# Moving the output-projection load, joining two transposes and splitting the gate/up tasks in a fused linear-attention and GEGLU kernel

## The chip, the cores and the metric

The kernel runs on one core of a Trainium2 chip. Its engines are TensorE (PE in the profile; its weight loads are the row PEld), VectorE (DVE), ScalarE (ACT), GpSimd (POOL) and SyncE (SP), which here only issues DMA transfers. The metric is device microseconds (us) of one execution; each version is told by the median of several runs.

## The reference

The input x has 2048 tokens of 448 numbers in bfloat16. The block is linear attention with 16 heads of 28 and then a gated MLP, each behind a layer norm without weights and each with a residual:

```python
def phi(t): return where(t > 0, t + 1, exp(t)) + 1e-6
q, k, v = split(layernorm(x) @ wqkv)          # 16 heads of 28
kv  = einsum("bhsd,bhse->bhde", phi(k), v)    # summed over all tokens
z   = phi(k).sum(tokens)
o   = (phi(q) @ kv) / (phi(q) @ z + 1e-6)
h   = x + o @ wo
g, u = layernorm(h) @ w_gate, layernorm(h) @ w_up      # 448 -> 1792
out = h + (gelu(g) * u) @ w_down                        # 1792 -> 448
```

Since kv and z are sums over all tokens, no token's o can be computed before all keys and values are there. That splits the program in two halves.

## The kernel before

**Tiles.** The tokens are 16 tiles t of 128. In the first half a tile is normed (`norm t`, on DVE for tiles 0 to 3, on POOL for the rest), transposed into `xnT`, and projected. Tiles 0 to 3 are transposed by TensorE (`tr0` to `tr3`, L495) and copied out of PSUM by ACT (`ev0` to `ev3`, L523); tiles 4 to 15 by a DMA transpose that SP issues (`xT4` to `xT15`, L526). Projection is `k t` and `v t`, each a task of 8 or 6 matmuls of 448 columns. Then ACT takes the exponential (`ek t`, L565), `cl t` clamps it on POOL (L566), `ph t` on DVE makes phi(k) of it (L568), `evv t` on ACT copies v (L570), and `acc t a/b` adds phi(k) times v into two PSUM banks. The queries are projected in eight pairs of tasks `qa c h`, `qb c h` (chunk c of four tiles, half h); ACT and DVE make phi(q) of them (`eq`, `rq`, `cq`, `pq`, L616 to L627).

**Second half.** `kz1` and `kz2` (DVE, L642 and L643) copy the finished sums. `nd t` multiplies phi(q) by them, `rd t` and `om t` divide (L654, L655), the result `o_sb` is transposed into `oT`, `wo t` multiplies by wo, `hr t` adds the residual (L660), layer norm follows, its result `hn` is transposed into `hnT`, and `gu v` computes gate and up for one or two blocks of 128 of the 1792 columns; ACT takes the gelu (`ge`, L830), DVE multiplies (`hm`, L832), and `down` multiplies by w_down. Tiles 0 and 1 take a short way: TensorE transposes o (`tro0`, `tro1`, L681) and hn (`trh0`, `trh1`, L702). The others go by DMA transpose in pairs: `nd t a/b`, `oT`, `wo t a/b`, `hT`. The MLP runs over token chunks of 2, 2, 4, 4 and 4 tiles: gu0 to gu6, gu7 to gu13 (256 columns a matmul, two column blocks a task), then 14 tasks of 512 columns for each chunk of four tiles.

**Half-array matmuls.** Most tasks use matmuls of 64 rows that come in pairs, one on the upper rows of the array (A), one on the lower (B), each into its own PSUM bank; the two run beside each other (`pe_pairs`, L430). The `b` task of a pair writes the same two banks with the row halves exchanged, and so waits until the `a` task has left the array. Tasks nd0, nd1, tro, wo0, wo1, trh and down12 to down15 use all 128 rows.

**What sets the order.** Every engine runs its tasks in a list written out by hand in `ORDERS`, one string for each of PE, ACT, DVE, POOL and SP. The graph works out which tasks a task depends on, and each engine waits by semaphores (`wait_ge`) at the head of the task, or in the middle of it for tasks whose later matmuls alone need something. SP's queue before is: the loads of x and wqkv, xT4 to xT15, four loads of wo (`dwo`, `dwo_t`, `dwo_u`, `dwo_s`, 336, 56, 56 and 336 KB), fourteen of gate and up (`dwg`, `dwu`, 224 KB each), oT2, oT3, the load of w_down, and so on. At the start PE runs 16 small and `WARM = 38` larger matmuls on ones (`warm1`, `warm0`, L454), whose result nobody reads, while x is on its way. These are the lines that the prediction's steps touch:

```python
G.add("pe", warm_fn(WARM), r=[b_ones], w=bank(0), name="warm0", dur=WARM * 0.107, key=-100.0)
prev = xts[-1:]                                  # wo's first load stands behind xT15
op("pool", lambda e: e.tensor_scalar(tm1[:, ie, :], e1[:, ie, :], 1.0 + EPS, 0.0, ALU.min, ALU.max), ...)   # cl t
pe_pairs("gu%d" % v, both(a, b), N, ...)         # one task of 28 matmuls
```

Of the kernel before, what the change touches and what calls it, by code (L numbers as in the profile page):

```python
# [213 lines left out]
def _c_act(n):  # L214
    return 0.05 + n / 1200.0
# [15 lines left out]
def bass_sequential_preLN__linear_attn_block__glu_gated_geglu__prompt_kernel(  # L231
# [13 lines left out]
    QCH = 512  # L245
    NQC = S // QCH
    N_PE_TR = 4
    STAT_GROUPS = [[0], [1], [2], [3]] + [[t, t + 1] for t in range(4, T, 2)]
    EV_DVE = cfg.get("ev_dve", ())
    N_DVE_NORM = cfg.get("n_dve_norm", 4)  # L250
    N_PE_A2 = 2
# [661 lines left out]
```

## Time and profile before

| | us |
|---|---|
| median of three runs | 196.68 (196.21 to 196.73) |
| the profiled execution, its own time | 196.7 |
| its span, first to last instruction | 194.9 |
| PE busy | 190.3 (98%) |
| DVE busy | 116.3 (60%) |
| ACT busy | 78.2 (40%) |
| POOL busy | 42.0 (22%) |

The profile is one execution. 1.8 us of its own time lie outside its span. Times in the rows count from the span's start. Rows of a timeline give the start, the length, the engine, the line, the operation, what it writes and reads, and how many instructions were merged; in brackets stands how long the engine was idle before, and what ended it. PE's matmuls are pipelined, so rows of the same engine overlap by some 0.2 us, and the distance from one row's start to the next is the better measure of what a task costs.

### The profile page before, as it was taken

How to read it: one execution, taken by the hardware profiler on the slowest of the kernel's cores; microseconds unless marked ns; L12 is line 12 of the kernel's file. 1: busy time of each engine (PE TensorE's matmuls, PEld its weight loads, DVE VectorE, ACT ScalarE, POOL GpSimd, SP SyncE). 2: the span in 40 equal slices, each digit the busy share in tenths (PEclk: the TensorE clock that was granted, in tenths of full speed). 3: DMA queues.
4: the chain of work that ended last, by engine and by line, in shares of the span. 5: the costliest groups of instructions: out<-in, count | busy, mean ns of one | idle time of the engine just before them, and what ended most of it. 6: DMA issues, size and time to landing. Idle time of an engine off the chain costs nothing.

```text
span 194.9 us, 5336 instructions
## 1 busy us (share of the span) xinstructions
PE 190.3 (98%) x2192; PEld 137.9 (71%) x2192; DVE 116.3 (60%) x301; ACT 78.2 (40%) x205; POOL 42.0 (22%) x90
## 2 busy tenths in 40 slices
PE   7999999999999999999999999999999999999994
PEld 7556658754588977976675577877778779899554
DVE  2989735368998946843967745756735443431512
ACT  3689866669784212220442441233232442411100
POOL 3099974300050310500500500500500000000000
PEclk9999999999999999999999999999999999999999
DMA  6944558999836052152062250172040000010111
GB/s 191 377 116 97 81 110 185 247 248 205 260 103 110 15 101 50 50 105 62 10 129 46 46 106 2 30 117 51 5 94 28 23 0 0 3 47 3 47 47 47
DMA packets 37256, 17.53 MB, mean 90 GB/s; under 512 B 28272, under 2 KB 36336, under 8 KB 37232
## 3 DMA queue, kind: packets, MB, share of 16 engines
q1 hardware_dynamic: 36352, 16.45, 36.8%
q10 hardware_dynamic: 880, 0.75, 1.2%
q8 instruction: 17, 0.28, 0.6%
q14 instruction: 7, 0.06, 0.1%
HBM read 8.72 MB, written 1.84 MB: 54 GB/s over the span
## 4 chain that ended last, share of the span: by engine, by line
PE 96%; issue 1%; ACT 1%; DVE 1%; POOL 0%; DVEq 0%; ACTq 0%; POOLq 0%
PE ps L430 87%; PE ps L780 6%; PE ps L454 2%; DVE x_sb L660 1%; PE ps L495 1%; ACT xn L617 1%; PE ps L681 0%; ACT xnT L523 0%; PE ps L672 0%; DVE x_sb L756 0%; POOL ones_bf L395 0%; POOL eps_t L398 0%; ACT pqT L616 0%; DVEq L196 0%; ACTq L196 0%
## 5 line engine op out<-in xcount | busy, mean ns | idle before, releaser
L430 PE MATMUL ps<-hnT,wgu_sb 64*128 64x512 bf16 (+1 forms) x980 | 90.4, 333 | 0.0
L430 PEld LDWEIGHTS ps<-hnT,wgu_sb 64*128 64x128 bf16 x980 | 64.5, 94 | 18.6 <-DVE hh L832 1.7
L830 ACT ACTIVATE gl<-ps 128x256 bf16<-128x256 f32 x112 | 36.9, 381 | 89.3 <-PE ps L430 88.2
L832 DVE TENSOR_TENSOR hh<-ps,gl 128x256 bf16<-128x256 f32 x112 | 42.5, 415 | 35.7 <-ACT gl L830 31.5
L430 PE MATMUL ps<-wd_sb,hh 64*128 64x448 bf16 x336 | 34.4, 349 | 0.0
L430 PEld LDWEIGHTS ps<-wd_sb,hh 64*128 64x128 bf16 x336 | 25.6, 94 | 6.2 <-DVE x_sb L756 0.2
L430 PE MATMUL ps<-wkv_sb,xnT 64*128 64x448 bf16 x192 | 22.4, 350 | 0.4 <-ACT xnT L523 0.4
L462 DVE BATCH_NORM_STATS2 st<-x_sb 128x6 f32<-128x448 bf16 x32 | 18.7, 611 | 2.6 <-DMA x_sb<-in_A_x_dram 2.6
L756 DVE TENSOR_TENSOR x_sb<-ps,x_sb 128x448 bf16<-128x448 f32 (+1 forms) x17 | 9.9, 591 | 16.6 <-PE ps L430 9.8
L474 POOL TENSOR_SCALAR ln<-mv 128x2 f32<-128x2 f32 x7 | 1.6, 223 | 75.0 <-DVE mv L463 74.9
L568 DVE SCALAR_TENSOR_TENSOR pk<-ps,tm 128x448 bf16<-128x448 f32 x16 | 9.8, 620 | 9.6 <-POOL tm L566 7.1
L430 PE MATMUL ps<-xnT,wq_sb 64*128 64x512 bf16 x112 | 14.9, 377 | 0.2 <-ACT xn L617 0.2
L430 PEld LDWEIGHTS ps<-wkv_sb,xnT 64*128 64x128 bf16 x192 | 10.1, 94 | 6.3 <-issue 0.8
L430 PE MATMUL ps<-wo_sb,oT 64*128 64x448 bf16 x98 | 12.1, 350 | 0.1
L660 DVE TENSOR_TENSOR x_sb<-ps,x_sb 128x448 bf16<-128x448 f32 x16 | 9.4, 618 | 4.6 <-PE ps L430 4.4
L780 PE MATMUL ps<-wd_sb,hh 128*128 128x448 bf16 (+1 forms) x70 | 10.8, 315 | 0.0
L566 POOL TENSOR_SCALAR tm<-e 128x448 bf16<-128x448 bf16 x16 | 8.9, 559 | 6.4 <-ACT e L565 5.5
L487 POOL TENSOR_SCALAR hn<-x_sb,nm,rs 128x448 bf16<-128x448 bf16 x14 | 10.0, 720 | 0.8 <-POOL rs L476 0.2
L565 ACT ACTIVATE e<-ps 128x448 bf16<-128x448 f32 x16 | 8.5, 541 | 3.5 <-PE ps L430 2.2
L780 PEld LDWEIGHTS ps<-wd_sb,hh 128*128 128x128 bf16 x70 | 6.7, 98 | 4.3 <-issue 0.4
L655 DVE TENSOR_TENSOR o_sb<-ps,rd 128x448 bf16<-128x448 f32 x16 | 9.4, 612 | 0.1
L570 ACT ACTIVATE v<-ps 128x448 bf16<-128x448 f32 x16 | 8.4, 542 | 2.1 <-PE ps L430 2.1
(69 smaller groups left out, 140.4 us busy)
## 6 DMA issues: line engine op xcount, KB each, us to landing
out_dram<-x_sb SPq DMA_DIRECT2D x15, 112.0 KB, 1.7
wgu_sb<-in_B_w_gate_dram SPq DMA_DIRECT2D x7, 224.0 KB, 6.1
wgu_sb<-in_B_w_up_dram SPq DMA_DIRECT2D x7, 224.0 KB, 6.4
wd_sb<-in_B_w_down_dram SPq DMA_DIRECT2D x1, 1568.0 KB, 8.3
x_sb<-in_A_x_dram SPq DMA_DIRECT2D x2, 448.0 KB, 5.3
wkv_sb<-in_A_wqkv_dram ACTq DMA_DIRECT2D x2, 336.0 KB, 3.7
x_sb<-in_A_x_dram SPq DMA_DIRECT2D x3, 224.0 KB, 4.2
wo_sb<-in_A_wo_dram SPq DMA_DIRECT2D x2, 336.0 KB, 4.4
```

Source lines behind the costliest of these rows:

```text
L430: ins = e.matmul(o_, l_, r_, start=s_, stop=p_, **kw)
L462: op("dve", lambda e: e.bn_stats(st[:, t, :], src_ap), [b_src], [b_st[t]], "%sbnst%d" % ("" if mv is mv1 else "h", t), 0.53, key, after=after)
L487: return lambda e: e.tensor_scalar(dst, src[:, t, :], nm[:, t:t + 1], rs[:, t:t + 1], ALU.add, ALU.mult)
L565: act_exp(lambda e: e.activation(e1[:, ie, :], oK, AF.Exp), bank(bk), [b_e1[ie]], "ek%d" % t, _c_act(D), kk)
L566: op("pool", lambda e: e.tensor_scalar(tm1[:, ie, :], e1[:, ie, :], 1.0 + EPS, 0.0, ALU.min, ALU.max), [b_e1[ie]], [b_tm1[ie]], "cl%d" % t ...
L568: op("dve", lambda e: e.scalar_tensor_tensor(pk[:, i, :, 0:GW], psK3, EPS, tm1[:, ie, :].rearrange("p (g e) -> p g e", g=NG), ALU.max, ALU ...
L655: op("dve", lambda e: e.tensor_tensor(o_sb[:, so, oc:oc + D].rearrange("p (a e) -> p a e", e=28), nd3[:, :, 0:28], rd[:, i, :].unsqueeze(2 ...
L660: op("dve", lambda e: e.tensor_tensor(h_sb[:, u, :], ps[:, b, 0:D], x_sb[:, u, :], ALU.add), bank(b) + [b_x[u]], [b_h[u]], "hr%d" % u, 0.5 ...
L756: op("dve", lambda e: e.tensor_tensor(x_sb[:, t, c0:c1], ps[:, bk, c0:c1], h_sb[:, t, c0:c1], ALU.add), bank(bk) + [b_h[t]], [bo], "out%d% ...
L780: ins = e.matmul(ps[:, bk, c0:c1], hh[:, j, hsl(t)], wd_sb[:, j, c0:c1], start=(j == 0), stop=(j == NJ - 1))
L830: G.add("act", lambda e, gi=gi, cs_=cs_, psG=psG: e.activation(gl[:, gi, cs_], psG[:, cs_], AF.Gelu_apprx_tanh), r=bank(BK_G[i]), w=[b_glh ...
L832: op("dve", lambda e, dst=dst, srcU=srcU, srcL=srcL: e.tensor_tensor(dst, srcU, srcL, ALU.mult), bank(BK_U[i]) + [b_glh], [b_ar[j_][t % HR ...
```

## The change

- `WARM` goes from 38 to 33.
- SP's queue: `dwo` and `dwo_t` stand behind xT9, `dwo_u` and `dwo_s` behind xT11; gate and up follow xT15 directly. `WO_AT = 3` lets wo's first load stand anywhere behind xT6.
- `cl14` and `cl15` run on DVE (`CL_DVE`).
- One task `tro0` takes the place of tro0 and tro1: it transposes o of both tiles by 16 transposes of 64 rows, A and B, into two banks; `evo0` and `evo1` each read both banks.
- In `trh` the wait for the copied columns (`wrap`) moves to the seventh transpose.
- The gate/up tasks of two column blocks (gu0 to gu13) become two tasks each, `gu v a` and `gu v b`, with 14 matmuls; their number in all, their banks and the work of ACT and DVE behind them stay.
- The five lists are written anew. Beside what the excerpts below show, PE's list has qa20 behind acc14a and down6 to down10 earlier among the gate/up tasks; ACT's has ek15 ahead of evv15 and rstd3 behind ek0 and ln4; POOL's has norm11 behind norm12; DVE's has pq8, pq12 and pq14 later, and hm33_0 behind hr14 and hr15; SP's has dout13 ahead of dout10, dout11, dout9 and dout12.

```diff
-    " qa20 acc13a acc14a qb20 acc14b acc15b acc15a qa11 nd0 nd1 qb11 qa30 nd2a tro0 nd2b qb30 qa21 tro1 qb21 wo1 wo0"
-    " qa31 wo2a qb31 wo2b trh1 trh0 nd4a nd4b gu1 gu0 gu3 gu2 gu5 wo4a wo4b gu4 nd6a gu7 nd6b gu6 down0a gu9 wo6a gu8"
+    " acc13a acc14a qa20 acc14b acc15b qb20 acc15a qa11 nd0 nd1 qb11 qa30 nd2a tro0 nd2b qb30 qa21 qb21 wo1 wo0 qa31"
+    " wo2a wo2b trh1 trh0 qb31 nd4a nd4b gu1a gu1b gu0a gu0b gu3a gu3b gu2a gu2b gu5a gu5b wo4a gu4a wo4b gu4b gu7a"
...
+    CL_DVE = cfg.get("cl_dve", (14, 15))
...
-    WARM = 38
+    WARM = 33
...
+    WO_AT = 3
...
-        prev = xts[-1:]
+        prev = xts[WO_AT:WO_AT + 1]
...
+        prev = prev + xts[-1:]
+
         for k in range(7):
...
-            op("pool", lambda e: e.tensor_scalar(tm1[:, ie, :], e1[:, ie, :], 1.0 + EPS, 0.0, ALU.min, ALU.max),
-               [b_e1[ie]], [b_tm1[ie]], "cl%d" % t, 0.53, kk)
+            op("dve" if t in CL_DVE else "pool", lambda e: e.tensor_scalar(tm1[:, ie, :], e1[:, ie, :], 1.0 + EPS, 0.0, ALU.min, ALU.max),
+               [b_e1[ie]], [b_tm1[ie]], "cl%d" % t, _c_dve(D, 4.0) if t in CL_DVE else 0.53, kk)
...
-            def ftro(e):
-                ins = None
-                for k in range(4):
-                    ins = e.transpose(tvo[:, k, :], o_sb[:, so, k * 128:(k + 1) * 128], ident[:])
-                return ins
-            G.add("pe", ftro, r=[b_o[so], b_ident], w=bank(bh), name="tro%d" % t, dur=_c_mm(128, 4), key=ka)
-            op("act", lambda e: e.activation(oT[:, so, :, :], tvo, AF.Identity), bank(bh), [b_oT[so]], "evo%d" % t, _c_act(512), ka)
+        def tro_first():
+
+            P, Q = FIRST_BK[0][1], FIRST_BK[1][1]
 
             def ftro(e):
                 ins = None
-                for k in range(4):
-                    ins = e.transpose(tvo[:, k, :], o_sb[:, so, k * 128:(k + 1) * 128], ident[:])
+                for t in (0, 1):
+                    for k in range(4):
+                        for b, rows in ((P, A_), (Q, B_)):
+                            ins = e.transpose(psb[:, b, (4 * t + k) * 64:(4 * t + k + 1) * 64], o_sb[rows, t % O_R, k * 128:(k + 1) * 128], ident[rows, rows])
                 return ins
+            G.add("pe", ftro, r=[b_o[0], b_o[1], b_ident], w=bank(P, Q), name="tro0", dur=0.054 * 8, key=-19.9, mode=64, rg={P: "A", Q: "B"})
+            for t in (0, 1):
+                tvo = psb[:, P:Q + 1, t * 256:(t + 1) * 256].rearrange("p b (k t) -> p k b t", t=64)
+                ov_ = oT[:, t % O_R, :, :].rearrange("p k (b t) -> p k b t", t=64)
+                op("act", lambda e, tvo=tvo, ov_=ov_: e.activation(ov_, tvo, AF.Identity), bank(P, Q), [b_oT[t % O_R]], "evo%d" % t, _c_act(512), -19.8)
...
-            G.add("pe", ftrh, r=[b_hn[sh], b_hnd[sh], b_ident], w=bank(bh), name="trh%d" % t, dur=_c_mm(128, 7), key=ka)
+            G.add("pe", ftrh, r=[b_hn[sh], (b_hnd[sh], 6), b_ident], w=bank(bh), name="trh%d" % t, dur=_c_mm(128, 7), key=ka, mw=True, pdt=_c_mm(128))
...
-                a, b = [], []
                 for jj in range(nj):
                     j = j0 + jj
+                    a, b = [], []
...
-                pe_pairs("gu%d" % v, both(a, b), N, [b_hnT[t % HR] for t in tiles] + [(x, 2 * k) for k, x in enumerate(b_wg)] + [(x, 2 * k + 1) for k, x in enumerate(b_wu)],
-                         [(b_ps[BK_G[i]], 0), (b_ps[BK_U[i]], 1)], kb, {BK_G[i]: "A", BK_U[i]: "B"})
+                    pe_pairs("gu%d%s" % (v, "ab"[jj] if nj > 1 else ""), both(a, b), N,
+                             [b_hnT[t % HR] for t in tiles] + [(x, 2 * k) for k, x in enumerate(b_wg)] + [(x, 2 * k + 1) for k, x in enumerate(b_wu)],
+                             [(b_ps[BK_G[i]], 0), (b_ps[BK_U[i]], 1)], kb + 0.01 * jj, {BK_G[i]: "A", BK_U[i]: "B"})
```

In SP's queue, from the last small load on (`pqT<-ones_bf`), before:

```order
L364 DMA pqT<-ones_bf 1x64x128
L526 DMA_TRANSPOSE xnT<-xn 128x4x128 x12
L364 DMA wo_sb<-in_A_wo_dram 128x3x448
L364 DMA wo_sb<-in_A_wo_dram 64x448 x2
L364 DMA wo_sb<-in_A_wo_dram 128x3x448
L364 DMA wgu_sb<-in_B_w_gate_dram 64x1792
```

and now (`xnT<-xn` are xT4 to xT15, `wo_sb` the four loads of wo):

```order
L367 DMA pqT<-ones_bf 1x64x128
L529 DMA_TRANSPOSE xnT<-xn 128x4x128 x6
L367 DMA wo_sb<-in_A_wo_dram 128x3x448
L367 DMA wo_sb<-in_A_wo_dram 64x448
L529 DMA_TRANSPOSE xnT<-xn 128x4x128 x2
L367 DMA wo_sb<-in_A_wo_dram 64x448
L367 DMA wo_sb<-in_A_wo_dram 128x3x448
L529 DMA_TRANSPOSE xnT<-xn 128x4x128 x4
L367 DMA wgu_sb<-in_B_w_gate_dram 64x1792
```

Six transposes stand behind loads that they stood ahead of, and the first load of gate and up follows the last transpose.

On PE, from nd0 and nd1 (`ps<-kvz,pqT` x8, 128 rows) to the first full-array matmuls of wo1, before (`xnT,wq_sb` are qa and qb, `ident,o_sb` is tro):

```order
L672 MATMUL ps<-kvz,pqT 128x116 x8
L430 MATMUL ps<-xnT,wq_sb 128x512 x14
L430 MATMUL ps<-kvz,pqT 128x116 x8
L681 MATMUL ps<-ident,o_sb 128x128 x4
L430 MATMUL ps<-kvz,pqT 128x116 x8
L430 MATMUL ps<-xnT,wq_sb 128x512 x14
L681 MATMUL ps<-ident,o_sb 128x128 x4
L430 MATMUL ps<-xnT,wq_sb 128x512 x6
L688 MATMUL ps<-wo_sb,oT 128x448 x3
```

and now:

```order
L676 MATMUL ps<-kvz,pqT 128x116 x8
L433 MATMUL ps<-xnT,wq_sb 128x512 x14
L433 MATMUL ps<-kvz,pqT 128x116 x8
L690 MATMUL ps<-ident,o_sb 128x64 x16
L433 MATMUL ps<-kvz,pqT 128x116 x8
L433 MATMUL ps<-xnT,wq_sb 128x512 x20
L706 MATMUL ps<-wo_sb,oT 128x448 x3
```

tro1 between qa21 and qb21 is gone, and the one tro0 stands between nd2a and nd2b.

On PE, from qa31 to the tasks behind wo4, before (`ident,hn` is trh, `kvz,pqT` x16 is nd4a and nd4b, `wo_sb,oT` are wo2 and then wo4, `hnT,wgu_sb` gate and up):

```order
L430 MATMUL ps<-xnT,wq_sb 128x512 x8
L430 MATMUL ps<-wo_sb,oT 128x448 x8
L430 MATMUL ps<-xnT,wq_sb 128x512 x6
L430 MATMUL ps<-wo_sb,oT 128x448 x6
L702 MATMUL ps<-ident,hn 128x128 x14
L430 MATMUL ps<-kvz,pqT 128x116 x16
L430 MATMUL ps<-hnT,wgu_sb 128x256 x140
L430 MATMUL ps<-wo_sb,oT 128x448 x14
L430 MATMUL ps<-hnT,wgu_sb 128x256 x28
```

and now:

```order
L433 MATMUL ps<-xnT,wq_sb 128x512 x8
L433 MATMUL ps<-wo_sb,oT 128x448 x14
L722 MATMUL ps<-ident,hn 128x128 x14
L433 MATMUL ps<-xnT,wq_sb 128x512 x6
L433 MATMUL ps<-kvz,pqT 128x116 x16
L433 MATMUL ps<-hnT,wgu_sb 128x256 x140
L433 MATMUL ps<-wo_sb,oT 128x448 x8
L433 MATMUL ps<-hnT,wgu_sb 128x256 x14
L433 MATMUL ps<-wo_sb,oT 128x448 x6
L433 MATMUL ps<-hnT,wgu_sb 128x256 x28
```

qb31 went from between wo2a and wo2b to behind trh0, and half of gu4 stands between wo4a and wo4b.

More of the change, by code (lines that the diff above doesn't have):

```diff
@@ L661, in res_h, with nd_first @@
             ln_stats(u, h_sb[:, u, :], b_h[u], st2, mv2, b_st2, b_mv2, ka)
-        def a2_first(t):
+        def nd_first(t):
             ka = -20.0 + 0.1 * t
-            bnd, bh = FIRST_BK[t]
-            so = t % O_R
+            bnd = FIRST_BK[t][0]
             def fnnd(e):
@@ L696, in a2_first, with ftrh @@
             tvh = psb[:, bh, 0:896].rearrange("p (k t) -> p k t", k=7)
-            def ftrh(e):
+            def ftrh(e, W):
                 ins = None
-                for k in (0, 1, 2, 4, 5, 6, 3):
+                for n, k in enumerate((0, 1, 2, 4, 5, 6, 3)):
+                    if n in (0, 6):
+                        W(n)
                     ko = k * 128 if k < 4 else (k - 4) * 128 + 64
@@ L837, in gu_chunk @@
             vcount[0] = v
+        for t in (0, 1):
+            nd_first(t)
+        tro_first()
         done = 0
```

5 lines of the change are left out of this document (4 added, 1 removed), and 91 rows, old and new, of the table ORDERS.

## The prediction

> **What bounds the kernel now.** I read the page first: the share of the span by engine, and the chain that ended last.
>
> ```profile
> PE 190.3 (98%) x2192; PEld 137.9 (71%) x2192; DVE 116.3 (60%) x301; ACT 78.2 (40%) x205; POOL 42.0 (22%) x90
> ...
> PE 96%; issue 1%; ACT 1%; DVE 1%; POOL 0%; DVEq 0%; ACTq 0%; POOLq 0%
> ```
>
> PE is busy for 98% of the span and is 96% of the chain. What can be won is the time before its first useful matmul and the few places where it waits. The chain in order of time says where these are:
>
> ```profile
> 10.51 27.04 PE ps L430 x336
> ...
> 48.05 1.03 ACT xn L617
> ...
> 52.26 1.17 DVE x_sb L660 x2
> ...
> 62.84 40.46 PE ps L430 x552
> ...
> 103.35 78.37 PE ps L430 x776
> ```
>
> Behind 62.84 PE runs on without a break that matters (40.46 and 78.37 us in single pieces), so from there a change of order wins nothing and can only lose. The time lies in three stretches: the start, 37 to 54 us, and wo4 at 62.
>
> **The start: five warm-up matmuls less.** The timeline of the start:
>
> ```profile
> 1.93 4.24 PE L454 MATMUL ps<-ones_bf 128*128 128x128 bf16 x38
> 5.21 0.37 DVE L486 TENSOR_SCALAR xn<-x_sb,mv,rs 128x448 bf16<-128x448 bf16 x1
> 6.10 0.96 PE L495 MATMUL ps<-ident,xn 64*128 64x64 bf16 x20
> 7.43 0.74 PE L430 MATMUL ps<-wkv_sb,xnT 64*128 64x448 bf16 x6 [0.36 <-ACT xnT L523]
> 9.76 0.75 PE L495 MATMUL ps<-ident,xn 64*128 64x64 bf16 x20
> 10.26 0.20 ACT L469 ACTIVATE rs<-ln 128x2 f32<-128x2 f32 x1
> 10.35 1.08 ACT L523 ACTIVATE xnT<-ps 128x512 bf16<-128x512 bf16 x2
> 10.99 0.31 PEld L430 LDWEIGHTS ps<-wkv_sb,xnT 64*128 64x128 bf16 x6 [0.26 <-ACT xnT L523]
> 11.00:20.00 9.00, 9.00 (x114) 5.15 (x114) 8.60 (x24) 8.22 (x27) 9.00 (x18) 1.00 0.41 83
> ```
>
> One warm-up matmul takes 4.24 / 38 = 0.11, five 0.53. But tr0 needs norm0, which ends at 5.21 + 0.37 = 5.58, so tr0 moves from 6.10 to about 5.65, and k0 from 7.43 to 6.98: 0.45 won. At k2 (10.99, idle 0.26) PE waits for ev2 (10.35). ACT's new list puts rstd3 ahead of it, at the price of rstd4, 10.35 - 10.26 = 0.09, so 0.35 arrives there. In the stretch from 11 to 20 (the last row: PE, PEld, DVE, ACT, POOL busy) POOL is busy for 9.00 of 9.00 us and DVE for 8.60, and PE gets its banks back only when they are done. POOL's share can begin some 0.25 earlier, as its input `ek1` does. Ends: 0 (POOL's row alone decides) and 0.45; I take 0.25.
>
> **wo between the transposes.** Nothing needs wo before wo1 at 47.02 (its row is below); what counts is who is moved past. SP's rows and the landing times of L526:
>
> ```profile
> 20.68 2.59 SPq L526 DMA_TRANSPOSE xnT<-xn  x2
> 23.47 1.19 SPq L526 DMA_TRANSPOSE xnT<-xn  x1
> 28.64 3.19 SPq L364 DMA_DIRECT2D wo_sb<-in_A_wo_dram  x4
> DMA to landing us min/median/max: 2.4/2.5/4.1
> 25.70 0.73 PE L430 MATMUL ps<-wkv_sb,xnT 64*128 64x448 bf16 x6
> 30.42 0.82 PE L430 MATMUL ps<-wkv_sb,xnT 64*128 64x448 bf16 x6
> ```
>
> xT10 is issued at 20.68 and lands 2.5 later, at 23.2; k10 reads it at 25.70. xT12 is issued at 23.47, lands near 26, and k12 reads it at 30.42. Four issues take 3.19. Two of them (1.9 with the long first one) now stand ahead of xT10, partly where SP waited anyway: I put xT10 at 22.0, landing at 24.5. All four stand ahead of xT12, and xT11 waits longer for norm11, which POOL now makes after norm12: xT12 at 25.9, landing at 28.4 to 30.0 (2.5 to 4.1). k10 and k12 come at 25.45 and 30.15. So the cover is 0.9 at k10 and 0.15 to 1.75 at k12, and I cost this at nothing; without the cover it is the first rival. Gate and up start behind xT15 without wo's 3.19 in between, so w_gate, w_up, oT2 and oT3 come no later.
>
> **37 to 41 us: cl14, cl15 and the order of acc.** The rows of POOL and DVE:
>
> ```profile
> 38.58 0.56 POOL L566 TENSOR_SCALAR tm<-e 128x448 bf16<-128x448 bf16 x1 [0.75 <-ACT e L565]
> 39.27 0.62 DVE L568 SCALAR_TENSOR_TENSOR pk<-ps,tm 128x448 bf16<-128x448 f32 x1 [0.68 <-PE ps L430]
> 40.62 0.63 DVE L642 TENSOR_TENSOR kvz<-ps,mask 113x448 bf16<-113x448 f32 x1 [0.73 <-PE ps L430]
> 41.24 0.42 DVE L618 TENSOR_SCALAR pqT<-pqT 112x1024 bf16<-112x1024 bf16 x1
> ```
>
> DVE's own clamp of 1024 numbers takes 0.42, so 448 take at most that; I take 0.35 against POOL's 0.56. With ek15 ahead of evv15 (0.4) and ph14 out of the way, ph15 comes some 0.9 earlier. Little of it counts: qa20 now waits for evv15, which is 0.4 later, and qb20 for qa20. Following the tasks one by one, the last acc leaves PE 0.2 earlier, kz1 (40.62) too. Won: 0.19; ends 0 and 0.5 (the 0.73 that DVE waits ahead of kz1, less what evv15 loses).
>
> **41 to 54 us: the joint transpose and qb31.**
>
> ```profile
> 43.78 0.40 PE L681 MATMUL ps<-ident,o_sb 128*128 128x128 bf16 x4
> 44.11 0.38 PE L430 MATMUL ps<-kvz,pqT 64*128 64x116 bf16 x8
> 45.94 0.40 PE L681 MATMUL ps<-ident,o_sb 128*128 128x128 bf16 x4
> 46.27 0.82 PE L430 MATMUL ps<-xnT,wq_sb 64*128 64x512 bf16 x6
> 47.02 0.74 PE L688 MATMUL ps<-wo_sb,oT 128*128 128x448 bf16 x3
> 49.21 1.04 PE L430 MATMUL ps<-xnT,wq_sb 64*128 64x512 bf16 x8 [0.19 <-ACT xn L617]
> 52.16 0.95 PE L702 MATMUL ps<-ident,hn 128*128 128x128 bf16 x14
> 53.47 0.82 PE L430 MATMUL ps<-kvz,pqT 49*128 49x116 bf16 x15 [0.21 <-DVE x_sb L660]
> 54.13 2.13 PE L430 MATMUL ps<-hnT,wgu_sb 64*128 64x256 bf16 x36
> ```
>
> tro0 and tro1 cost 44.11 - 43.78 = 46.27 - 45.94 = 0.33 each. Sixteen half-size transposes at the pace of tr2 and tr3 (20 in 0.75, 0.037 each) cost 0.6 at most. qb21 now follows qa21 at once and waits until it has left the array, 0.1 to 0.2, where tro1 stood; wo1 no longer waits for an evo1 that ACT makes between two other tasks. Together wo1 comes at 46.7, 0.34 before its 47.02. qa31 waits for rq10 (0.19 in the row, 48.05 + 1.03 in the chain), which ACT starts behind qb21: it moves by the same 0.34. wo2b, now right behind wo2a, waits about 0.2 that qb31 used to cover; qb31 in its new place covers the 0.43 from 53.04 to 53.47 that nd4a waits for hr3. gu1 comes at 53.72 in place of 54.13: 0.41 in all, 0.22 beside the 0.19 above. Ends: 0 (the later ge1, behind eq14 and the table load, holds gu3) and 0.7 (nothing waits).
>
> **gu4a between wo4a and wo4b.** wo4a and wo4b without cover, and wo6b, which has other work ahead of it:
>
> ```profile
> 61.77 1.81 PE L430 MATMUL ps<-wo_sb,oT 64*128 64x448 bf16 x14
> 63.42 0.82 PE L430 MATMUL ps<-hnT,wgu_sb 64*128 64x256 bf16 x12
> 74.88 0.74 PE L430 MATMUL ps<-wo_sb,oT 64*128 64x448 bf16 x6
> 75.45 0.74 PE L430 MATMUL ps<-wd_sb,hh 64*128 64x448 bf16 x6
> ```
>
> The 14 matmuls of wo4 take 63.42 - 61.77 = 1.65; the 6 of wo6b take 75.45 - 74.88 = 0.57, and 14 at that pace 1.33. Won: 0.30; ends 0 (oT4 or oT5 late) and 0.32. Splitting the tasks adds no matmul and no wait that the first half has not ended: nothing. The wait inside trh: nothing, since normh0 is the later one and wrap0 is made while trh1 runs.
>
> **What can be lost.** In the long gate/up stretch PE has no slack to give, and DVE's new list puts hm33_0 behind hr14 and hr15, so gu35 may wait some 0.1. dout13 ahead of four older outputs delays these, but they leave before out14 is ready, 2.65 us of down14 later (70 matmuls of the last tasks in 10.75, a fifth of them each).
>
> ```profile
> 181.72 10.75 PE ps L780 x70
> ```
>
> **The sum.** 0.25 + 0.19 + 0.22 + 0.30 - 0.10 = 0.86. The profiled execution took 196.7, as the median of the runs does (196.68), so the changed kernel takes 195.8.
>
> **Rivals.** *The transposes come late.* For it: one transpose landed 4.1 after its issue, and cover at k12 is 0.15 with such a landing. Against: the median is 2.5. It decides from the point where xT12 lands after 30.15. With another 1.0 of delay (the loads of wo drawn out in front of it), plus as much at k10 beyond its 0.9, the kernel loses 1.0 to 1.6: 196.8 to 197.4, slower than before.
>
> *The array's clock.* The 128 columns of a warm-up matmul take 0.11, those of trh 0.95 / 14 = 0.07, with pipeline; k0 at 7.43 has the fast pace (6 matmuls in 0.74). So the array runs at a slow pace until some point before 7.43, though the clock column reads 1.00 (row 11.00:20.00 and all others). If the release depends on how much work came before, five matmuls less may leave k0, v0, k1 and v1 slow: 28 matmuls of 27.04 / 336 = 0.08 (the chain's row), at double price 2.3 more, less some 0.5 for the waits among them that they would fill. 195.8 + 1.8 = 197.6. The Trainium skill (TensorE: Matmul & The Clock Gate, Part 1) says that the array starts at half rate and that the budget is some 3.4 us of time in a free-running window, not a number of matmuls; by it the release comes either at its old time, which costs k0 at most half of the 0.45 it gained, or a window later. The trace agrees that the pace doubles before 7.43 and cannot show what sets the moment.
>
> *The vector engines hold the loop.* POOL's 9.00 of 9.00 speaks for it. Then the start wins nothing, and part of the later terms goes into other waits: 0.2 to 0.5 won in place of 0.86, 196.3.
>
> **How the numbers follow.** Forecast 0.62, its own range 195.2 to 196.2; vector engines 0.14; late transposes 0.11; clock 0.06; more than 1.5 won, since waits further on shrink as well, 0.07. About 0.3% (0.59 us) is what a measurement of this kernel can tell from no change. Faster: 0.58 of the forecast's and the last case, 0.65. Within: 0.04 of the forecast, the vector case, 0.04 of the late transposes, 0.22. Slower: the rest of these and the clock, 0.13. The range 195.2 to 196.9 leaves out the clock, half of the late transposes and part of the last case.
>
> **What would show it.** Right: tr0 at 5.6 and k0 at 7.0; no PE idle ahead of k10 and k12; kz1 0.4 to 0.5 earlier than 40.62, wo1 0.6 earlier than 47.02, gu1 near 53.5; wo4a and wo4b without idle time between. Wrong: PE idle at k10 or k12 with a DMA as releaser; k0 and v0 at twice their length; k4 to k9 at their old times; idle of PE behind 62 us, released by DVE's hm or by a DMA.

## The result, and the profile after

The changed kernel takes 197.01 us (median of 21 runs, 196.44 to 199.23), the kernel before 196.37 beside it (21 runs, 196.06 to 196.73): a ratio of 1.0037, 95% interval 1.0024 to 1.0049. It is slower, by 0.64 us. The forecast was 195.8, and the time lies outside its range of 195.2 to 196.9. The profiled execution took 196.78 with a span of 195.1.

The page of the changed kernel, shares by engine, the chain, and the group of the k and v matmuls:

```profile
PE 189.6 (97%) x2195; PEld 123.9 (64%) x2195; DVE 117.4 (60%) x303; ACT 77.6 (40%) x205; POOL 41.1 (21%) x88
...
PE 91%; DMA 4%; ACT 1%; issue 1%; DVE 1%; SPq 0%; DVEq 0%
...
L433 PE MATMUL ps<-wkv_sb,xnT 64*128 64x448 bf16 x192 | 22.9, 350 | 0.5 <-DMA xnT<-xn 0.4
```

DMA had no share of the chain before. It has 4% now, and most of the idle time ahead of the k and v matmuls is released by the transposes of xn. The chain in order of time says what the 4% are:

```profile
1.25 3.35 DMA x_sb<-in_A_x_dram
...
25.80 5.10 DMA xnT<-xn
30.90 0.14 issue
31.04 6.95 PE ps L433 x86
...
53.76 49.33 PE ps L433 x693
...
103.13 78.69 PE ps L433 x768
```

The larger part is tile 12's transpose: issued at 25.80, 5.10 us until it lands, and k12 behind it at 31.04. The 3.35 at the start are the load of x, which stands on the chain in place of the warm-up matmuls. The timeline of PE shows the places of the forecast (the last two rows are the first matmuls of wo12a and of down12):

```profile
2.24 3.40 PE L457 MATMUL ps<-ones_bf 128*128 128x128 bf16 x33
5.80 0.41 PE L498 MATMUL ps<-ident,xn 64*128 64x64 bf16 x10 [0.16 <-DVE xn L489]
6.59 0.41 PE L498 MATMUL ps<-ident,xn 64*128 64x64 bf16 x10 [0.38 <-DVE xn L489]
7.01 0.74 PE L433 MATMUL ps<-wkv_sb,xnT 64*128 64x448 bf16 x6
...
25.52 0.82 PE L433 MATMUL ps<-wkv_sb,xnT 64*128 64x448 bf16 x6
31.04 0.74 PE L433 MATMUL ps<-wkv_sb,xnT 64*128 64x448 bf16 x6 [0.36 <-DMA xnT<-xn]
47.05 0.74 PE L706 MATMUL ps<-wo_sb,oT 128*128 128x448 bf16 x3
53.98 1.25 PE L433 MATMUL ps<-hnT,wgu_sb 64*128 64x256 bf16 x20
61.73 1.02 PE L433 MATMUL ps<-wo_sb,oT 64*128 64x448 bf16 x8
62.48 1.03 PE L433 MATMUL ps<-hnT,wgu_sb 64*128 64x256 bf16 x14
63.25 0.83 PE L433 MATMUL ps<-wo_sb,oT 64*128 64x448 bf16 x6
114.70 0.98 PE L433 MATMUL ps<-wo_sb,oT 64*128 64x448 bf16 x8
181.76 1.50 PE L800 MATMUL ps<-wd_sb,hh 128*128 128x448 bf16 x7
```

The same two last places in the kernel before:

```profile
114.92 0.97 PE L430 MATMUL ps<-wo_sb,oT 64*128 64x448 bf16 x8
181.65 1.69 PE L780 MATMUL ps<-wd_sb,hh 128*128 128x448 bf16 x8
```

And the queue of SP with the landing times of the twelve transposes of xn:

```profile
20.20 1.38 SPq L367 DMA_DIRECT2D wo_sb<-in_A_wo_dram  x2
21.68 2.62 SPq L529 DMA_TRANSPOSE xnT<-xn  x2
24.35 1.40 SPq L367 DMA_DIRECT2D wo_sb<-in_A_wo_dram  x2
25.80 5.66 SPq L529 DMA_TRANSPOSE xnT<-xn  x4
DMA to landing us min/median/max: 2.4/3.0/5.1
```

Read from the timelines as starts of tasks, the time went and came in these stretches (a positive number is won):

| stretch | before | after | won |
|---|---|---|---|
| start to k6 | 18.74 | 18.56 | 0.18 |
| k10 to v15 (k12 waits) | 10.84 | 11.37 | -0.53 |
| v15 to nd0 | 4.90 | 4.93 | -0.03 |
| nd0 to gu1 | 12.69 | 12.16 | 0.53 |
| gu1 to down0 | 14.29 | 14.07 | 0.22 |
| down0 to wo12a | 46.50 | 46.65 | -0.15 |
| wo12a to down12 | 66.73 | 67.06 | -0.33 |

That is 0.93 won and 1.04 lost (k6 to k10 takes 6.96 in both): 0.11 between the two profiles, where the medians differ by 0.64. The two profiled executions are not alike in one thing, the array's pace at the start. Before, k0 came at 7.43 in the profiled execution, whose 196.7 is among the slower of its 21; in two later runs whose first tasks are those of the kernel before (e2 and e14 below) the pace doubled during the warm-up matmuls already, and k0 came at 7.15 and 7.12. In the changed kernel's profile it doubled early too. From k0 to the end of the span the kernel before takes 194.94 - 7.43 = 187.51 and the changed one 195.05 - 7.01 = 188.04. That difference, 0.53, is nearer to the 0.64 of the medians: of the 0.42 that k0 seems to have won, 0.11 to 0.14 is what is left against e2 and e14. These are single executions: in e12, e13 and e15 to e17, with the new order of the start and 38 warm-up matmuls, k0 comes between 6.93 and 7.35, so the change's own share is not settled.

### The profile page after: what moved, and what is told of

The parts are those of the page before. It is cut to its first block, busy times and chain, and to the rows that moved or that the text cites. A ratio compares the mean times of both kernels' runs of the same rounds, so it can differ in the third digit from the quotient of the medians.

```text
span 195.1 us, 5340 instructions
## 1 busy us (share of the span) xinstructions
PE 189.6 (97%) x2195; PEld 123.9 (64%) x2195; DVE 117.4 (60%) x303; ACT 77.6 (40%) x205; POOL 41.1 (21%) x88
## 4 chain that ended last, share of the span: by engine, by line
PE 91%; DMA 4%; ACT 1%; issue 1%; DVE 1%; SPq 0%; DVEq 0%
PE ps L433 84%; PE ps L800 6%; DMA xnT<-xn 3%; DMA x_sb<-in_A_x_dram 2%; ACT xn L622 1%; PE ps L498 0%; PE ps L722 0%; DVE st L465 0%; ACT e L570 0%; PE ps L676 0%; DVE xn L489 0%; SPq L367 0%; DVE x_sb L776 0%; ACT ln L470 0%; ACT v L575 0%
## 5 line engine op out<-in xcount | busy, mean ns | idle before, releaser
L433 PE MATMUL ps<-hnT,wgu_sb 64*128 64x512 bf16 (+1 forms) x980 | 91.6, 333 | 0.0
L433 PEld LDWEIGHTS ps<-hnT,wgu_sb 64*128 64x128 bf16 x980 | 55.1, 94 | 30.0 <-DVE hh L853 4.5
L433 PE MATMUL ps<-wd_sb,hh 64*128 64x448 bf16 x336 | 35.2, 349 | 0.0
L433 PEld LDWEIGHTS ps<-wd_sb,hh 64*128 64x128 bf16 x336 | 23.7, 94 | 8.0 <-DVE hh L853 0.3
L433 PE MATMUL ps<-wkv_sb,xnT 64*128 64x448 bf16 x192 | 22.9, 350 | 0.5 <-DMA xnT<-xn 0.4
L484 POOL TENSOR_SCALAR nm<-mv 128x2 f32<-128x2 f32 x13 | 2.9, 227 | 39.3 <-DVE mv L466 38.9
```

Source lines behind the costliest of these rows:

```text
L433: ins = e.matmul(o_, l_, r_, start=s_, stop=p_, **kw)
```

## The experiments

Four theories stand in the expectations. L: transposes land late, those of xn where wo is moved ahead of them, or those of o. W: 33 warm-up matmuls leave the array at half pace into the first tiles in some executions. R: the new order behind 62 us, and above all behind 114, costs time. G (e8): the fill between wo4a and wo4b wins by itself. F (from e9 on): what delays a transpose is the load of instructions on which it falls. All runs stand beside runs of the kernel before on the same chip; "high" counts runs above 197.5, which the kernel before never reached. The ratio compares all runs and not the two medians, so that high runs weigh in it (e4, e11).

| run | median | before beside it | ratio (95%) | runs, high |
|---|---|---|---|---|
| e1 change, wo back | 197.12 | 196.54 | 1.0030 (1.0010 to 1.0051) | 12, 5 |
| e2 before, wo moved | 196.73 | 196.54 | 1.0019 (1.0004 to 1.0035) | 12, 3 |
| e3 change, 38 warm-ups | 197.27 | 196.54 | 1.0037 (1.0020 to 1.0054) | 12, 3 |
| e4 before, 33 warm-ups | 196.50 | 196.54 | 1.0019 (0.9996 to 1.0041) | 12, 4 |
| e5 change, wo back, 38 | 197.23 | 196.46 | 1.0039 (1.0020 to 1.0057) | 12, 4 |
| e6 change, old late order | 197.19 | 196.46 | 1.0054 (1.0029 to 1.0080) | 12, 3 |
| e7 before, 24 warm-ups | 197.86 | 196.46 | 1.0078 (1.0050 to 1.0107) | 7, 6 |
| e8 before, halved gate/up | 197.31 | 196.46 | 1.0040 (1.0028 to 1.0052) | 5, 0 |
| e9 change, 8 wide warm-ups | 196.83 | 196.59 | 1.0025 (1.0009 to 1.0040) | 12, 2 |
| e10 change, 66 narrow ones | 197.86 | 196.59 | 1.0060 (1.0038 to 1.0082) | 12, 8 |
| e11 change, half of wo back | 196.44 | 196.59 | 1.0009 (0.9990 to 1.0028) | 12, 3 |
| e12 a mixed version | 197.30 | 196.59 | 1.0039 (1.0027 to 1.0051) | 6, 0 |
| e13 three causes undone | 196.58 | 196.50 | 1.0007 (0.9992 to 1.0021) | 12, 0 |
| e14 before, new late order | 196.53 | 196.50 | 1.0004 (0.9994 to 1.0013) | 12, 0 |
| e15 two causes undone | 196.50 | 196.50 | 1.0000 (0.9990 to 1.0010) | 12, 0 |
| e16 e13, o transposes first | 196.19 | 196.28 | 0.9993 (0.9979 to 1.0008) | 12, 0 |
| e17 e16, all of wo back | 196.21 | 196.28 | 0.9994 (0.9985 to 1.0003) | 12, 0 |

**One part undone, one part alone (e1 to e4).**

```diff
 e1, on the changed kernel (SP)
- xT9 dwo dwo_t xT10 xT11 dwo_u dwo_s xT12 xT13 xT14 xT15 dwg0
+ xT9 xT10 xT11 xT12 xT13 xT14 xT15 dwo dwo_t dwo_u dwo_s dwg0
 e2, on the kernel before (SP): the same the other way round
 e3, on the changed kernel
-    WARM = 33
+    WARM = 38
 e4, on the kernel before
-    WARM = 38
+    WARM = 33
```

> The changed kernel, with the four loads of wo back behind xT15 and all else kept. Theory L (the transposes come late: in the trace of the changed kernel xT12 lands at 30.90 and k12 starts at 31.04, 0.7 after PE was ready for it): k12 no longer waits, the time falls by 0.6 to 0.8 against the changed kernel, to 196.2 to 196.4. Theory W (what costs is the shorter warm-up, where the array's clock is released late): the time stays near 197.0. Theory R (the other reordering, behind 62 us, costs it): the time stays near 197.0.

> The kernel before, with only the loads of wo moved between the transposes. Theory L: xT12 lands at 29 to 31 where k12 comes at 30.4, so 0 to 0.6 slower than before, 196.4 to 197.0, with more spread. Theories W and R: as before, 196.4.

> The changed kernel, with 38 warm-up matmuls in place of 33. Theory W: the spread of its runs (196.4 to 199.2) shrinks to about 0.7, its median falls to 196.6 to 196.9, no run stands above 197.6. Theory L: median 197.0 to 197.2, since what the start gives back is partly time that k12 waits for xT12 anyway; the spread stays. Theory R: 197.2.

> The kernel before, with 33 warm-up matmuls in place of 38. Theory W: some runs much slower than 197, median 196.4 to 196.8. Theories L and R: 0 to 0.4 faster than before, 196.0 to 196.4, with before's spread.

No single part is the whole. With wo back (e1) k12 no longer waits (30.64, tile 12's transpose landed at 27.82), but the time does not fall. The wait has moved to wo2a, which reads the transposes of o tiles 2 and 3; PE's timeline and the landing of those transposes in e1:

```profile
50.49 2.16 PE L433 MATMUL ps<-wo_sb,oT 64*128 64x448 bf16 x14 [0.45 <-DVE st L465]
DMA to landing us min/median/max: 4.1/4.6/5.0
```

The releaser that is named, a statistic of DVE, had long been done: the transposes landed at 50.40 and 50.80. In the changed kernel they take 2.4 to 2.5 and land at 48.08 and 49.40; in e1 the last gate/up block ahead of them lands at 49.84 in place of 47.34. So wo between the transposes of xn delays these, and wo behind them delays those of o. This profiled execution took 197.59 and is one of the five high ones of e1, though its k0 to k2 run at full pace: a high run need not be one at half pace. wo moved alone (e2) leaves k12 at 30.19 without a wait in its profile; the ratio is 1.0019, and the three high runs among its twelve have no profile and stay unexplained. Five warm-up matmuls more do not mend the changed kernel (e3, k12 at 31.68, three runs high). Five less in the kernel before (e4) split its runs in two: eight at 196.3 to 196.66, four at 197.87 to 198.16.

**The array's pace (e5 and e7).**

```diff
 e5: e1 with
-    WARM = 33
+    WARM = 38
 e7, on the kernel before
-    WARM = 38
+    WARM = 24
```

> The changed kernel with wo put back behind xn tile 15's transpose and with 38 warm-up matmuls. Theory W (33 warm-up matmuls leave the array at half pace into the first tiles in some executions, about 1.5 us each time): the upper group that both kernels with 33 showed in a third of their executions (197.6 to 198.2) is gone; every execution lies within 0.8 us of the fastest, and as k0 starts some 0.3 to 0.5 later than with 33 (7.74 against 7.26 to 7.43), the median is 196.7 to 197.2. Theory L (the upper group is late transposes, of xn where wo is moved and of o where it is not): a third of the executions stays 1.2 us or more above the fastest, and k12 or wo2a waits in the profile. Theory R (the order behind 114 us costs 0.3): wo12a to down12 stays 67.06 as in the changed kernel, against 66.73 before, here and in every kernel with the new late order.

> The kernel before with 24 warm-up matmuls. Theory W: the array goes to full pace only after a stretch of work of a certain length, so with 24 (2.6 us at 107 ns) more executions than the third of 33's fall into the upper group, half or more of them at 197.5 to 198.5, and a profile of one shows matmuls of k0 to k2 at twice their duration (about 400 ns for 128x448 in place of some 200). Rival: the upper group has nothing to do with the warm-up (late transposes): the median stays at 196.4 to 196.6 and a third or fewer lie above 197.5, with full pace from k0 on in the profile.

e7 answers clearly: six of seven runs are high. Stages of 3.4 us of its profiled execution (PE, PEld, DVE, ACT, POOL busy; then the granted clock):

```profile
4.20:7.60 3.40, 1.78 (x31) 1.08 (x30) 2.78 (x8) 1.99 (x6) 0.00 (x0) 1.00 1.10 373
7.60:11.00 3.40, 3.34 (x29) 1.26 (x24) 2.95 (x11) 2.35 (x9) 0.98 (x3) 0.53 1.08 358
```

The array is busy for 1.78 of 3.40 us in the one stage, and in the next the granted clock is 0.53 and k2 starts at 12.11 in place of 11.02. The Trainium skill (TensorE: Matmul & The Clock Gate, Part 1) describes a free-running window of 3413 ns that decides on half or full rate; the trace agrees: from 7.83 to 11.24 us the granted clock is 0.50, and in the 3.41 us on either side 1.00. That a stage with 1.78 us of work was not enough is what the run adds.

Half pace in the first tiles was caught in e10 and e11 too, but of another kind: there the pace had not doubled at all before 10.7 us. The clock column says nothing (1.00), and the matmuls themselves show it. First e11, its warm-up and its k and v matmuls from 7.2 to 10.7 us, then the changed kernel's from 7.2 to 10.7:

```profile
2.24 3.70 PE L457 MATMUL ps<-ones_bf 128*128 128x128 bf16 x33
...
L433 PE MATMUL ps<-wkv_sb,xnT 64*128 64x448 bf16 x16 | 3.3, 560 | 0.2 <-ACT xnT L526 0.2
```

```profile
L433 PE MATMUL ps<-wkv_sb,xnT 64*128 64x448 bf16 x24 | 2.8, 351 | 0.1
```

The 33 warm-up matmuls of e11 take 3.70 us, 0.11 each to the last (3.40 in the changed kernel's profile, where the last few are twice as fast). Then it is 560 ns in place of 351 for the same matmul: k1 starts at 10.04, 2.83 behind k0 where it is 1.57, and that run took 199.07. e5 did not come out as W had it: four of twelve runs are still high with 38 warm-up matmuls, and its profiled execution (197.39) shows the full pace but a late wo2a. Its warm-up starts at 2.24 like the changed kernel's. The start itself is moved by the change, which the prediction had not seen: GpSimd's list now has the memset of ones behind three others, so that the warm-up starts at 2.24 in place of 1.93. In e8 and e12 to e17, all with 38 warm-up matmuls from 1.93 on, none of 71 runs is high, though e16's slowest (197.49) only just; e2, which has the same warm-up, has its three. So W is borne out by e4 and e7 against the kernel before; it does not explain e1's profiled run, and e2's stay open. That the later start alone makes e3's and e5's was not tried apart.

**The late order (e6 and e14) and the halved gate/up tasks (e8).**

```diff
 e6, on the changed kernel: behind wo12b the order before, all engines (PE shown)
- wo12b gu28 nd14a gu29 nd14b down4b gu30 gu31 down6a gu33 wo14a
+ wo12b gu29 nd14a gu28 nd14b gu31 down4b gu30 gu33 gu32 wo14a
 e14, on the kernel before: the same the other way round
 e8, on the kernel before: gate/up tasks of one column block, and (PE)
- gu5 wo4a wo4b gu4 nd6a gu7 nd6b gu6 down0a
+ gu5a gu5b wo4a gu4a wo4b gu4b nd6a gu7a gu7b nd6b gu6a gu6b down0a
```

> The changed kernel with the order before of everything behind wo12b (behind about 118 us) on all five engines. Theory R (the new late order of gate/up and down tasks costs time): wo12a to down12 falls from 67.06 to 66.73, and the median by 0.33, from 197.01 to about 196.7. If the 0.33 is not the order's but comes from what happened ahead of it (skew between the array's two halves, buffers held longer), it stays at 67.06 and the median at 197.0.

> The kernel before with the new order behind wo12b alone. Theory R (the order's own): wo12a to down12 67.0 to 67.1 in place of 66.73, median 0.3 higher than before, 196.8 to 196.9, with the narrow spread of the kernel before. If the loss comes from what stands ahead of it, it stays at 66.7 to 66.8 and the median at 196.5.

> The kernel before with one part of the change alone: gate/up tasks of one column block, and the first block of gu4 between the two halves of wo4; all else in the order before. Theory G (the fill between wo4a and wo4b is worth what the changed kernel showed from gu1 to down0a, 14.08 against 14.29): 0.2 faster, median 196.3, down0a 0.2 earlier than 68.42 and the gain kept to the end. Rival (the vector engines hold the gate/up loop, so the array waits there later): down0a earlier, but gu11 or down2a back on the old times, median 196.5.

The old late order gives back half of the 0.33 in the profile (wo12a to down12 66.89), none of it in the median. The new late order alone, in the kernel before, costs nothing that can be measured:

```profile
114.64 0.97 PE L430 MATMUL ps<-wo_sb,oT 64*128 64x448 bf16 x8
181.43 1.88 PE L780 MATMUL ps<-wd_sb,hh 128*128 128x448 bf16 x9
```

181.43 - 114.64 = 66.79 against 66.73, ratio 1.0004 (0.9994 to 1.0013). Theory R falls as the order's own doing. The 0.33 needs the new order both ahead of 118 us and behind it; PE shows no idle time in it in either kernel, and how it arises stays open.

e8 shows that gu4a between wo4a and wo4b is not worth anything by itself. PE's timeline of e8:

```profile
62.57 1.02 PE L431 MATMUL ps<-hnT,wgu_sb 64*128 64x256 bf16 x14
63.34 0.82 PE L431 MATMUL ps<-wo_sb,oT 64*128 64x448 bf16 x6
...
65.41 0.38 PE L431 MATMUL ps<-kvz,pqT 64*128 64x116 bf16 x8 [0.49 <-DVE x_sb L661]
```

wo4b ends later, so does h of tiles 4 and 5 on DVE, and nd6a, behind gu4b, waits 0.49 for its bank: down0a comes at 68.89 in place of 68.42. The changed kernel has nd6a between gu7a and gu7b, where half a gate/up task covers that wait (65.34, no idle), and there the fill pays: down0a at 68.05, 14.07 behind gu1, where e8 has 14.72.

**What delays a transpose (e9 to e11).**

```diff
 e9, on the changed kernel: 8 warm-up matmuls of 512 columns for 33 of 128
-                    ins = e.matmul(ps[:, 0, 0:128], ones_bf[:], ones_bf[:], start=True, stop=True)
+                    ins = e.matmul(ps[:, 0, 0:512].rearrange("p (a b) -> p a b", a=4), ones_bf[:], ones_bf[:].unsqueeze(1).to_broadcast([128, 4, 128]), start=True, stop=True)
 e10: 66 of 64 columns
+                    ins = e.matmul(ps[:, 0, 0:64], ones_bf[:], ones_bf[:, 0:64], start=True, stop=True)
 e11, on the changed kernel (SP)
- xT9 dwo dwo_t xT10 xT11 dwo_u dwo_s xT12 xT13 xT14 xT15 dwg0
+ xT9 dwo dwo_t xT10 xT11 xT12 xT13 xT14 xT15 dwo_u dwo_s dwg0
```

> The changed kernel with its 33 warm-up matmuls of 128 columns replaced by 8 of 512 columns (the same columns, so the same length at either pace), which takes 25 matmuls and their weight loads out of TensorE's instruction stream. Theory F: the transposes of xn tiles that are in flight while the profile shows 16 KB on the instruction queue (28 to 30 us in the changed kernel) take 4 to 5 us in place of 2.5 to 3, and in the changed kernel it is tile 12's that is hit, which is waited for. With fewer instructions ahead the fetch comes 1 to 2 us later, tile 12's transpose lands by 29.5 in place of 30.90, k12 starts without idle about 0.5 earlier relative to k10, and the median falls by 0.4 to 0.5, to about 196.5. Rival (theory L: it is wo's own 784 KB ahead of it in the queues that delays tile 12's transpose): it lands near 30.9 as in the changed kernel, k12 waits 0.5 to 0.7, and the median stays at 197.0.

> The changed kernel with 66 warm-up matmuls of 64 columns in place of 33 of 128 (the same columns), which puts 33 more matmuls and their weight loads into TensorE's instruction stream. Theory F: the 16 KB on the instruction queue comes 1 to 2 us earlier than in the changed kernel, at 26.5 to 28, and hits the transposes of xn tiles 11 and 12 (3.5 to 5 us each), while tiles 14 and 15 go back to about 2.5; k12 waits 0.2 to 0.7 still, since tile 12's is issued at 25.8, so the median stays at 196.8 to 197.1. Theory L: landing times as in the changed kernel, tile 12's at 30.9, tiles 13 to 15 at 31.7 to 32.7.

> The changed kernel with only the first half of wo (392 KB) between the transposes, behind xn tile 9, and the second half behind tile 15. Theory L: with no bytes of wo between tiles 11 and 12, and tile 12's transpose issued 1.25 us earlier (24.5 in place of 25.8), it lands at 27 to 28.5, k12 starts without idle; gate/up weights are issued some 0.6 us later than in the changed kernel and o's transposes land at 49 or earlier, so that wo2a does not wait: the loss of 0.5 at k12 goes and no other takes its place, median 196.5 to 196.7. Rival: moving the second half back delays o's transposes as it did with all of wo moved back (50.2 to 50.8), wo2a waits 0.3 or more and the median stays at 197.0 or above.

In the changed kernel the instruction queue has 16 KB in the stages 10 to 11, 19 to 20 and 28 to 29 us. The last of these, in its view of DMA, 28 to 29 us; the second row is the transposes whose issue falls in that stage, with their median time to landing:

```profile
q8 instruction: 1, 0.02, 8.9%
...
xnT<-xn SPq DMA_TRANSPOSE x2, 4.3
```

With 25 matmuls less ahead (e9) the same loads come at 13, 23 and 32 us. The stage 23 to 24 of e9:

```profile
q8 instruction: 1, 0.02, 5.8%
...
xnT<-xn SPq DMA_TRANSPOSE x1, 4.1
```

The slow transposes move with them. From issue to landing, in us (tiles 4, 8, 9, 10, 11, 12, 15): 2.8, 4.2, 3.2, 2.7, 3.4, 5.1, 2.5 in the changed kernel; 4.1, 2.6, 2.5, 4.5, 4.1, 3.4, 4.2 in e9. Tiles 8 and 9 are released from the load at 19, tiles 10 and 11 caught by that at 23, and 15 by that at 32. Tile 12 lands at 29.46, 1.44 earlier, with the same bytes of wo ahead of it. So F holds and the rival, wo's bytes alone, does not. But the 16 KB are not all: tile 12 still takes 3.4 in e9 with no such load beside it, and tile 10 takes 3.8 in e10 and 4.1 in e11 with none either, issued 1.2 behind wo's first loads; PE waits for it there, 0.81 and 1.02. Beside most of these, as beside tile 12 before (3.3), 8 KB come on another instruction queue (q14). What wo's bytes and what the 8 KB add was not told apart; the load's part of tile 12's 5.1 is some 1.7 by an estimate from e9 (5.1 less 3.4). The time follows only in part (196.83), because tile 10 is hit instead: k10 starts at 26.04 in place of 25.52, and k12 at 30.89. e10's profiled execution ran its first tiles at half pace (k1 10.08), which puts k6 1.7 us later, so the load meant to come earlier than 28 came at 30; tile 12, 13 and 14 (4.6, 4.3 and 3.5 us) are again those beside the load, at 30. It is no test of F.

With only the first half of wo moved (e11) the median is 196.44, 0.15 below the kernel before beside it where the changed kernel is 0.64 above, and seven of twelve runs lie at 196.13 to 196.45. It still has 33 warm-up matmuls, and three high runs, which keep its ratio at 1.0009. By the medians the other 0.39 MB and the two issues ahead of tile 12 carry most of the loss; e11's one profile is of a half-pace execution and cannot show it.

**The account put together (e12, e13, e15 to e17).**

```diff
 e15, on the changed kernel: e11 and
-    "eps mhalf opad ones mones ident mask_a
+    "ones eps mhalf opad mones ident mask_a
-    WARM = 33
+    WARM = 38
 e13: e15 and e6
 e12: e13, with all of wo behind xT15, and on SP
- dwg5 dwu5 dwg6 dwu6 oT2 oT3 dwd
+ oT2 oT3 dwg5 dwu5 dwg6 dwu6 dwd
 e16: e13, and on SP
- dwg5 dwu5 dwg6 dwu6 oT2 oT3 dwd
+ dwg5 dwu5 oT2 oT3 dwg6 dwu6 dwd
 e17: e16, with all of wo behind xT15
```

> A version that takes from the change what the runs showed to help and undoes the rest: wo behind xn tile 15 as before, the transposes of o tiles 2 and 3 issued ahead of the last two pairs of gate/up weight blocks, 38 warm-up matmuls with the memset of ones first on GpSimd as before, the order before behind wo12b; kept are the joint o transposes, the halved gate/up tasks with gu4a between wo4a and wo4b, and the order of the first 118 us. By the terms: k0 at 7.15 to 7.43 as before, k0 to gu1 46.4 to 46.6 (no wait at k12, none at wo2a) against 46.70, gu1 to wo12a 60.72 against 60.79, behind it 66.8 against 66.73: 0.1 to 0.4 below the kernel before, median 196.1 to 196.3 with the narrow spread of the kernel before (under 0.8 us). If the last weight blocks, issued some 9 us later, come too late, gu1 waits in its fifth to seventh block and the median is 196.8 or more.

> The changed kernel with all three causes undone and the rest kept: the second half of wo behind xn tile 15, 38 warm-up matmuls with the memset of ones first on GpSimd, the order before behind wo12b. By the terms: k0 at 7.15 to 7.43 as before, gu1 46.4 later as in the runs without a wait (53.6 to 53.8 against 54.13), wo12a 60.72 behind it, down12 66.8 to 66.9 behind that: 0.2 to 0.4 below the kernel before, median 196.1 to 196.3, and no execution above 197.0, since 38 warm-up matmuls from 1.93 us on leave none at half pace. If a cause is missing, the median is 196.6 or more.

> The changed kernel with the second half of wo behind xn tile 15, 38 warm-up matmuls and the memset of ones first, and its own late order kept. Theory R: 0.15 to 0.3 above the same kernel with the old late order, 196.3 to 196.6, wo12a to down12 67.0 to 67.1; no execution above 197.2. If the late order costs nothing of its own, the two agree within 0.1.

> e13 with the transposes of o tiles 2 and 3 issued ahead of the last pair of gate/up blocks (dwg6, dwu6). If the late o transposes are what is still lost: they land at 48 to 49.3, wo2a takes 0.59 again, gu1 starts 46.4 to 46.6 behind k0 (46.98 in e13), the last gate/up pair lands at 51.5 to 53 and is not waited for; median 196.1 to 196.3, 0.2 to 0.4 below the kernel before. If it is not: gu1 stays near 54.0 or waits for the last pair, and the median at 196.5 or above.

> e16 with all of wo behind xn tile 15, as before the change. If the place of wo matters only through the transposes that it delays, and o's no longer stand behind the weights, then tile 10's to 12's transposes land a little earlier than in e16, nothing waits for wo itself (wo1 starts at 46.3, wo lands by 38), and the time agrees with e16 within 0.15: 196.1 to 196.3. If o's transposes are still late behind the weights, which are all issued later, wo2a waits 0.2 to 0.4 and the median is 0.2 to 0.4 above e16's.

By its runs e15 closes the account of the loss: with the second half of wo behind tile 15 and the warm-up as before, the changed kernel is level with the kernel before (1.0000, 0.9990 to 1.0010). In its profile k12 follows k11 without a wait. The old late order on top (e13) adds nothing. Neither wins the 0.2 to 0.4 that the terms promised, and the reason is e1's again; wo2 and the landing of o's transposes in e15:

```profile
49.93 2.16 PE L433 MATMUL ps<-wo_sb,oT 64*128 64x448 bf16 x14
DMA to landing us min/median/max: 3.5/3.9/4.3
```

and in e16, where they are issued ahead of the last pair of gate/up blocks:

```profile
49.85 1.74 PE L433 MATMUL ps<-wo_sb,oT 64*128 64x448 bf16 x14
DMA to landing us min/median/max: 2.4/2.5/2.5
```

0.42 less, as in the changed kernel's own row (1.74 in sum there too), and gu1 at 53.73. The last weight pair lands at 52.19 and is not waited for. Two pairs behind the transposes (e12) are too many: the last lands at 55.60, and PE waits for it:

```profile
55.65 3.01 PE L433 MATMUL ps<-hnT,wgu_sb 64*128 64x256 bf16 x52 [0.68 <-DMA wgu_sb<-in_B_w_up_dram]
```

e16 and e17 are the best versions found, 196.19 and 196.21 beside 196.28; the intervals include 1, so they are not shown to beat the kernel before. In e17's profile k0 to the end takes 194.26 - 6.93 = 187.33, against 187.51 before and 188.04 in the changed kernel. e16 and e17 agree: once o's transposes do not stand behind the last pair of weights, it does not matter whether half of wo or all of it stands behind tile 15. The change's own place for wo was not tried with them.

## Why the prediction was wrong

**The step that failed: wo between the transposes, costed at nothing.** Its issue times were right: tile 10 at 21.68 (forecast 22.0), tile 12 at 25.80 (25.9). Its landing was not. The bound "28.4 to 30.0" took the slowest landing of the profile before, 4.1 us, as the worst that could come; tile 12 took 5.1 and landed at 30.90, behind the 30.15 at which k12 was due. What made that 4.1 was not asked. The slowest before were tile 9 (4.1) and tile 15 (3.7), in flight while 16 KB came on the instruction queue at 19 and 28 us, and nobody waited for them; tile 12's own took 3.3 and landed at 26.74, where the prediction read the median into it ("near 26"). The change put tile 12 onto the load at 28. PE waits 0.36 at k12, and k10 to v15 takes 0.53 more. The rival that the prediction named for it is the case that came in its sign (PE idle at k12 with a DMA as releaser), and had a chance of 0.11. That the time, 197.01, also lies in its 196.8 to 197.4 is in part luck: it priced 1.0 to 1.6 at k10 and k12 by wo's loads, where k10 did not wait, a load of instructions had a part, and nearly half of the loss came behind 68 us.

**The start.** k0 at 7.01 (forecast 6.98) is the right number by luck. The later start of the warm-up was missed, and much of the 0.45 was the moment at which the pace doubles, which differs from execution to execution; against e2 and e14 it is 0.11 to 0.14. Nor is it the warm-up that k0 waits for now: it stands behind tr1, which waited 0.38 for norm1, and that for the load of x. The price, not seen, is the executions that run their first tiles at half pace: three of 21 of the changed kernel are above 197.5 (they have no profile; e11's is of such a start), and 24 warm-up matmuls make it six of seven. The clock rival had the mechanism and the price (28 matmuls at double price; 1.3 measured from k0 to k1 in e11) and took it for all or nothing. It is a chance in each run. By the sentence of the Trainium skill (TensorE: Matmul & The Clock Gate, Part 1: a budget of time in a free-running window) the release would come at its old time or a window later. Both are seen: at 5.2 in the changed kernel's profile, at 10.7 in e10 and e11. e7 shows a third way, a release and then a fall back for 3.4 us.

**37 to 41 us.** kz1 came at 41.15, 0.53 later than 40.62. Of this 0.35 is there at v15 already, behind the late k12, and 0.10 is that the new list puts kz2 ahead of kz1. From v15 to nd0 nothing was won (4.93 for 4.90), where 0.19 was forecast, though DVE's own clamp took 0.28, less than the 0.35 costed; e15, without a wait at k12, has 4.93 too. The forecast gain was not there.

**41 to 54 us.** nd0 to gu1 fell by 0.53, more than the 0.22 forecast: the joint transposes and qb31 behind trh0 are worth it (which of them how much was not tried apart), and e16 shows the same 12.16 us without k12's wait ahead of it. wo1 at 47.05 stood where it did before only because everything ahead was 0.4 later.

**wo4.** 0.22 from gu1 to down0, where 0.30 was forecast for the fill, and no idle between wo4a and wo4b as said. e8 shows that the term had a condition that the working left out, nd6a half a task later.

**What can be lost behind 62 us.** gu35 did not wait for hm33_0 (its term of 0.10 was nothing), but 0.15 and 0.33 went elsewhere, without a wait that the profile names. By e14 the late order alone is free; why the 0.33 comes with both orders new stays open.

The sum of the gains, 0.93, thus came out near the 0.96 that the prediction added up, but as a sum of errors that cancel: 0.53 for 0.22 in one stretch, nothing for 0.19 in another, and a start that is partly chance. It fell on the costs: 0.53 from k10 to v15, 0.03 up to nd0 and 0.48 behind down0, where it had 0.10.

## What to carry to other kernels

Where a transfer is moved in a queue, bound its landing by asking what was beside the slowest one in the trace, and not by the slowest itself: here a load of instructions, whose moment follows the place in the program, was beside it, and the moved transfer landed on that load. Compare two profiles from the first useful matmul on, since the moment at which the array's pace doubles is drawn anew in each execution; and do not pay for an earlier start with the warm-up that keeps that moment early. Bytes taken from ahead of one transfer stand ahead of the next that is waited for (xn's transposes here, then o's), so a queue is checked to its end.

## What the runs showed of the hardware

- Of the eleven transposes of xn that were in flight beside a load of 16 KB on the instruction queue (changed kernel and e9), ten took 3.2 to 5.1 us and one 2.8; the quick ones take 2.4 to 2.7. The load's moment moves with the number of matmuls ahead: 19 and 28 us became 23 and 32 with 25 fewer. Some take 3.2 to 4.1 without that load (tiles 12 and 14 in e9, tile 10 in e11).
- In e7 the array, at full pace, fell back to half for 3.4 us after a stage in which it was busy for 1.78 of 3.40 us; in e4 it kept the pace that it reached at 3.9 us, with 2.10 us of work in the next 3.41. The clock column can read 1.00 while matmuls take 560 ns in place of 351 (e11).
- A transpose behind weight loads in SP's queue lands some 0.5 us behind the last of them: that of o tile 2 took 2.4 us with the last pair of blocks issued behind it (e16), and 3.5, 4.3 and 5.0 with that pair ahead of it and landing at 48.45 (before), 49.26 (e15) and 49.84 (e1).
